# A linear-attention block in front of a gated unit: the product of k and v stands in TensorE, q streams through it, and x is born as [channel, token]

## The chip, the core and the metric

The kernel runs on one core of a Trainium2 chip. The metric is the device time of one execution in microseconds. A core has five engines with an instruction queue each: TensorE (PE in the profile, with its weight loads shown apart as PEld), VectorE (DVE), ScalarE (ACT), GpSimd (POOL) and SyncE (SP), which here only starts transfers. An engine takes its instructions in the order in which they were written, and waits at a semaphore where one needs another engine's result.

## What is computed

```python
def _attn_ref(q, k, v, g_norm):                       # (8, 8, 576, 64): batch, head, token, channel
    kv = np.einsum('bhsd,bhse->bhde', k, v)           # 64 x 64 for each head
    out = np.einsum('bhsd,bhde->bhse', q, kv)
    rms = np.sqrt(np.mean(out * out, axis=-1, keepdims=True) + 1e-06)
    return out / rms * g_norm

# x: (8, 576, 512), the heads side by side; w_val, w_out: (512, 512); conv_w: (5, 512)
def _moe_ref(x, w_val, conv_w, w_out):
    xp = np.concatenate([np.zeros((B, K - 1, D)), x], axis=1)
    gate_pre = sum(conv_w[k] * xp[:, k:k + S, :] for k in range(K))
    gate = 1.0 / (1.0 + np.exp(-gate_pre))
    return (gate * (x @ w_val)) @ w_out
```

All is in fp32 on the chip. q, k, v and g_norm come in fp32, the three weights in fp64, which the kernel narrows itself. `g_norm` and the root of 64 are folded into the weights, so that what is left of the norm is x times (sum of squares + 64 eps) to the power -1/2, for each token and head.

## The kernel before

A batch has 576 tokens and 512 channels. The second half of the work wants x with channels on the partitions, as `xT[128, 4, 576]` with a halo of four blocks in front of it, because the causal convolution then is four shifted multiply-adds along the free dimension. The first half makes x with tokens on the partitions. The steps of a batch:

- `load_half`, `load_tails`, `load_q` and `load_q_rows` bring k, v and q in through SP's queue. `kv_product` (L408) makes kv for two heads at a time, one in output columns 0 to 63 and one in 64 to 127 of TensorE's array. `kv_copy` (L418) puts each pair on the diagonal of a 128x128 block, `kvbd`.
- `turn_q` (L431, L434) turns q in blocks of 32 by 32 on DVE; for the first two batches `turn_q_rows` (L446) and `sort_q` do it on TensorE and ScalarE.
- `raw_product` (L485): for each of five chunks of tokens (four of 128, one tail of 64) four products in which 128 tokens of q stand as weights and `kvbd`, 128 columns, streams. The result is [token, channel] in one PSUM bank of two that have the tag `raw`; the bank is held until x has been made from it.
- `square` (L499, ScalarE), `sums` (L507, a reduction on DVE), `powers` (L513, `pow` on GpSimd) give the factor of each token and head; `normalise` multiplies with it, on DVE for batches 0 to 2 (L528), on ScalarE with eight instructions for a chunk (L524) from batch 3 on.
- x is turned to channels on partitions: with transposes on TensorE (`turn_x`, L538) and a copy (`keep_x`, L545) for the first two batches and every tail; else with block transposes on DVE (`turn_blocks`, L553) and four transfers from GpSimd's queue for each quarter (`move_blocks`, L561). `halo` (L568, GpSimd) fills the four blocks in front of it.
- the gate: `gate_start` (L572, ScalarE), four `gate_tap` (L578, DVE, each 128x576), `gate_end` (L585, the sigmoid on ScalarE), four times for a batch.
- the value product with w_val: `val_product` (L590) as eight groups of four plain products for the first two batches, from batch 2 on `val_fast` (L640), Strassen's scheme with seven products out of eight, whose partial results `x_sums` (DVE) and `val_keep` (ScalarE copies and DVE adds) make and collect. `gated` (L603) multiplies the gate in.
- the output product: `out_product` (L671, and L678 for the tails of two batches) or `fast_product` (L735), Strassen again, with `token_sums` and `fast_keep`; `store` sends the rows out.

The first products of the kernel wait for loads. `keep_warm` (L397) puts products of the identity into TensorE's queue in that time.

The order of the instructions on every engine comes from a planner that runs when the program is built. Each step has an engine, a time that its author expects (`"PE", 0.905`), a wished start, the steps it needs, and the buffers it takes and frees. `order` picks again and again the step that can start first. `SHIFTS` moves the wished starts of single steps. PSUM's eight banks are dealt out as `kv` 1, `raw` 2, `tp` 1 and `mm` 4. So the program holds the work of about three batches at once: while one batch's output product runs, the next one's value product and the one after's attention lie between its groups.

## Time and profile before

| | us |
|---|---|
| median of three runs | 333.09 (332.76 to 333.61) |
| the profiled execution, its own time | 333.21 |
| its span, first to last instruction | 331.4 |

| group | instructions | busy us | mean ns |
|---|---|---|---|
| raw products (L485), full chunks | 256 | 34.1 | 279 |
| raw products (L485), tails | 64 | 5.4 | 286 |
| transposes of x on TensorE (L538) | 48 | 8.1 | 277 |
| squares on ScalarE (L499), all | 40 | 22.5 | 561 |
| reductions on DVE (L507), all | 40 | 25.2 | 630 |
| powers on GpSimd (L513), all | 40 | 67.7 | 1697 |
| x on ScalarE (L524) | 180 | 39.6 | 342 |
| block transposes of x on DVE (L553) | 24 | 16.7 | 700 |
| transfers of x's blocks (L561) | 96 | 52.9 | 557 |

The clock granted to TensorE has a mean of 0.999 of the full one. An fp32 product shows as two MATMUL records and two LDWEIGHTS records. A record's duration reaches from its start to the end of a pipeline that the next record has entered long before, so the durations of a group overlap with those of the next: what a group takes of TensorE's time is read from the distance between starts. In the timeline a row is a merged run: start, length, engine, line, operation, tiles, shapes, count.

### The profile page before, as it was taken

What the parts mean: (1) busy time and instruction counts of PE and PEld (TensorE: products, weight loads), DVE (VectorE), ACT (ScalarE), POOL (GpSimd) and SP (SyncE); (2) the same over time, 40 slices, a digit from 0 to 9 for tenths busy, and PEclk for the clock granted to TensorE, in tenths of its full rate; (3) what the DMA queues carried; (4) which work ended last, traced back from release to release, by engine and by line L of the source; (5) the groups of instructions that cost most, each with busy time, mean ns of one, the idle gap of its engine ahead of it and who ended that gap; (6) DMA issues with size and microseconds to landing.
All of it is one profiled execution on the core that took longest, in us unless ns stands there. A gap on an engine that the chain in (4) does not pass through costs nothing.

```text
span 331.4 us, 6416 instructions
## 1 busy us (share of the span) xinstructions
PE 318.4 (96%) x2193; PEld 244.5 (74%) x2193; DVE 268.8 (81%) x479; ACT 185.8 (56%) x497; POOL 135.2 (41%) x178
## 2 busy tenths in 40 slices
PE   4989999999999999999999999999999999999993
PEld 4988877878755747587778758787885888888752
DVE  3277689799999729999999999999896697999601
ACT  3646965874365667675347848763676543534220
POOL 3006325303347969802568247777223274000000
PEclk9999999999999999999999999999999999999999
DMA  6999897597866886772976899465201235211233
GB/s 205 303 224 355 232 338 204 149 257 217 267 177 176 229 236 163 172 230 71 297 172 164 209 265 278 107 148 131 66 2 32 63 64 122 72 32 34 63 79 79
DMA packets 46014, 55.37 MB, mean 167 GB/s; under 512 B 15754, under 2 KB 36254, under 8 KB 45982
## 3 DMA queue, kind: packets, MB, share of 16 engines
q1 hardware_dynamic: 42558, 48.41, 53.6%
q0 software_dynamic: 3072, 6.30, 8.4%
q10 hardware_dynamic: 352, 0.26, 0.4%
q8 instruction: 17, 0.28, 0.4%
q14 instruction: 15, 0.12, 0.1%
HBM read 39.21 MB, written 9.44 MB: 147 GB/s over the span
## 4 chain that ended last, share of the span: by engine, by line
PE 76%; DVE 8%; DMA 7%; SPq 4%; ACT 2%; issue 2%; POOL 1%; DVEq 0%; ACTq 0%; POOLq 0%
PE va L640 12%; PE a L735 10%; PE raw L485 9%; PE out L671 8%; PE cb L735 8%; PE val L590 8%; PE vc L640 6%; PE out L678 4%; PE kv L408 4%; DVE gate L578 4%; PE vb L640 3%; DMA k<-in_k_dram 2%; DMA w_wval<-in_moe_w_val_dram 2%; PE xTps L538 2%; DMA vl<-in_v_dram 2%
## 5 line engine op out<-in xcount | busy, mean ns | idle before, releaser
L513 POOL TENSOR_TENSOR rt<-ss,mhalf 128x8 f32<-128x8 f32 (+1 forms) x40 | 67.7, 1697 | 113.4 <-DVE ss L507 113.4
L578 DVE SCALAR_TENSOR_TENSOR gate<-xT,cwT,gate 128x576 f32<-128x576 f32 x128 | 98.8, 808 | 0.1
L561 POOL DMA_DIRECT2D xT<-y x96 | 52.9, 557 | 20.8 <-PE vc L640 7.5
L524 ACT ACTIVATE x<-raw,rt 128x64 f32<-128x64 f32 x180 | 39.6, 342 | 7.5 <-POOL rt L513 7.5
L485 PEld LDWEIGHTS raw<-kvbd,qT 128*128 128x128 f32 (+1 forms) x320 | 35.4, 180 | 8.4 <-issue 4.7
L485 PE MATMUL raw<-kvbd,qT 128*128 128x128 f32 (+1 forms) x320 | 39.1, 280 | 0.9 <-DVE x L528 0.6
L507 DVE TENSOR_REDUCE ss<-sq 128x8 f32<-128x520 f32 (+1 forms) x40 | 25.2, 630 | 11.3 <-ACT sq L499 10.8
L590 PE MATMUL val<-xT,wval 128*128 128x288 f32 x128 | 33.2, 409 | 0.0
L499 ACT ACTIVATE sq<-raw 128x512 f32<-128x512 f32 (+1 forms) x40 | 22.5, 561 | 18.5 <-PE raw L485 18.2
L671 PE MATMUL out<-wout,gv 128*128 128x512 f32 x64 | 28.5, 595 | 0.0
L590 PEld LDWEIGHTS val<-xT,wval 128*128 128x128 f32 x128 | 23.5, 190 | 5.8
L640 PE MATMUL va<-xs,vsum 128*128 128x288 f32 x96 | 27.3, 407 | 0.0
L603 DVE TENSOR_TENSOR gv<-gv,gate 128x576 f32<-128x576 f32 x32 | 23.5, 747 | 4.1 <-ACT gate L585 1.8
L585 ACT ACTIVATE gate<-gate 128x576 f32<-128x576 f32 x32 | 21.5, 690 | 8.9 <-DVE gate L578 8.6
L572 ACT ACTIVATE gate<-xT,cwT 128x576 f32<-128x576 f32 x32 | 24.1, 778 | 1.6 <-DVE gv L603 1.1
L735 PE MATMUL a<-wsum,sums 128*128 128x256 f32 x96 | 24.9, 381 | 0.0
L408 PEld LDWEIGHTS kv<-v,k 128*64 128x64 f32 x512 | 17.6, 137 | 6.6 <-issue 4.6
L408 PE MATMUL kv<-v,k 128*64 128x64 f32 x512 | 20.6, 226 | 1.3 <-DMA vl<-in_v_dram 1.2
L671 PEld LDWEIGHTS out<-wout,gv 128*128 128x128 f32 x64 | 11.8, 190 | 13.2 <-issue 12.4
L640 PEld LDWEIGHTS va<-xs,vsum 128*128 128x128 f32 x96 | 18.0, 190 | 4.7
L744 DVE TENSOR_TENSOR ot<-cb,ot 128x256 f32<-128x256 f32 x24 | 10.0, 416 | 13.8 <-ACT ot L748 9.5
L553 DVE STREAM_TRANSPOSE y<-x 128x512 f32<-128x512 f32 x24 | 16.7, 700 | 4.2 <-ACT x L524 4.2
(109 smaller groups left out, 561.7 us busy)
## 6 DMA issues: line engine op xcount, KB each, us to landing
q<-in_q_dram SPq DMA_DIRECT2D x96, 140.0 KB, 4.1
out_dram<-ot SPq DMA_DIRECT2D x140, 64.0 KB, 1.7
v<-in_v_dram SPq DMA_DIRECT2D x16, 512.0 KB, 5.3
k<-in_k_dram SPq DMA_DIRECT2D x16, 512.0 KB, 7.0
xT<-y POOLq DMA_DIRECT2D x96, 64.0 KB, 2.8
q<-in_q_dram SPq DMA_DIRECT2D x4, 512.0 KB, 6.9
w_wval<-in_moe_w_val_dram SPq DMA_DIRECT2D x4, 512.0 KB, 7.8
w_wout<-in_moe_w_out_dram SPq DMA_DIRECT2D x4, 512.0 KB, 6.8
```

Source lines behind the costliest of these rows:

```text
L408: nc.tensor.matmul(kvp[r * D:(r + 1) * D, hp, :], st["k", b, half][:, h, j, :] if j < NJ else kl[:, 2 * hp + r, :], st["v", b, half][:, h, ...
L485: nc.tensor.matmul(raw[row * m:(row + 1) * m, col * P:(col + 1) * P], st["qT", b][:, hp, c * P:c * P + m], kv_bd[b % 2][:, hp, :], start=T ...
L507: nc.vector.reduce_sum(out=ss[:, 0:n], in_=st["sq", b, c][:, 0:n], axis=AX.X)
L513: nc.gpsimd.tensor_tensor(out=rt[:, 0:n], in0=st["ss", b, c][:, 0:n], in1=mhalf[:, 0:n], op=ALU.pow)
L524: nc.scalar.activation(out=x[:, cols], in_=st["raw", b, c][:, cols], func=AF.Copy, scale=st["rt", b, c][:, h:h + 1])
L561: nc.gpsimd.dma_start(out=xTs[b % 2][i * TB:(i + 1) * TB, :, first:first + P], in_=y[a * TB:(a + 1) * TB, i])
L572: nc.scalar.activation(out=gate[:], in_=xTs[b % 2][:, jt, HALO:SX], func=AF.Copy, scale=cwT[:, K - 1, jt:jt + 1])
L578: nc.vector.scalar_tensor_tensor(out=gate[:], in0=xTs[b % 2][:, jt, tap * TB:tap * TB + S], scalar=cwT[:, tap, jt:jt + 1], in1=gate[:], op ...
L590: nc.tensor.matmul(val[:], wval[:, kc, jt * P:(jt + 1) * P], xTs[b % 2][:, kc, HALO + n * SV:HALO + (n + 1) * SV], start=(kc == 0), stop=( ...
L640: nc.tensor.matmul(st[bank, "val", b, mj][:], weights_[:, k], tokens()[:, k], start=(n in (0, 1, 3) and k == 0), stop=(k == NK // 2 - 1), ...
L671: nc.tensor.matmul(po[:], gv[:, jt, first:first + P], wout[:, jt, :], start=(jt == 0), stop=(jt == NK - 1),)
L735: nc.tensor.matmul(st[bank, i, p], tokens()[:, k], weights_[:, k], start=(n < 2 and k == 0), stop=(k == NK // 2 - 1), skip_group_check=True)
```

## The change

- kv is kept as it comes from PSUM, `kvs[128, 4, 64]`, two heads above each other, instead of on diagonals. `head` deals the heads out so that the slots fit.
- `raw_product` swaps the operands: a head's 64x64 kv stands in TensorE, q streams in 288 columns (half of the tokens). A group of four products has its operands in both halves of the rows and its results in both halves of the columns, and two PSUM banks as its result. There are four groups for a batch: two halves of the tokens (`g`), two pairs of channel blocks (`p`). The result is [channel, token].
- `keep_raw` (ScalarE) copies it straight into `xT`; `square` (ScalarE) squares it from there.
- `sums`: four products with `fold`, a 128x32 matrix of ones, add the squares over a head's channels and leave each head's sum on 16 partitions. `root` (ScalarE, Sqrt), `inverse` and `exact` (DVE: a reciprocal and three scalar_tensor_tensor, of which the last ones are a Newton step) make the factor.
- `spread`: two products of 32 rows with `spread_` lead each head's factor to its 64 channels, and `normalise` (DVE) multiplies `xT` with it in place.
- `turn_x`, `keep_x`, `turn_blocks` and `move_blocks` are gone, and `turn_q` is one transpose instead of two.
- the tag `raw` is one tile of two banks instead of two tiles of one bank. It holds a raw group, a spread factor, or the sums of an output product at the end.
- the value products need `xT` by halves and pairs, not by chunks. All wished starts in `SHIFTS` are others.

```diff
@@ -200,30 +205,29 @@
     loads = ctx.enter_context(tc.tile_pool(name="loads", bufs=2))
     work = ctx.enter_context(tc.tile_pool(name="work", bufs=2))
     psum = ctx.enter_context(tc.tile_pool(name="psum", bufs=1, space=bass.MemoryType.PSUM))
-    BANKS = {"kv": 1, "raw": 2, "tp": 1, "mm": 4}
+    BANKS = {"kv": 1, "raw": 1, "tp": 1, "mm": 4}
 
     def ps(kind, shape, name):
         return psum.tile(shape, FP32, tag=kind, bufs=BANKS[kind], name=name)
 
     plan = Planner({
-        "k0": 1, "k1": 1, "v0": 1, "v1": 1, "tails": 2, "q": 3, "w64": 3, "y": 2, "wexp": 2,
-        "kv": 1, "kvbd": 2, "qT": 2, "tp": 1, "raw": 2, "mm": 4, "sq": 2, "ss": 3, "rt": 3,
-        "x": 2, "xT": 2, "gate": GATES, "xs": 4, "gv": GVS, "ot": 3,
-    }, by_batch=("tails", "kvbd", "xT", "gv"))
+        "k0": 1, "k1": 1, "v0": 1, "v1": 1, "tails": 2, "q": 3, "w64": 3, "wexp": 2,
+        "kv": 1, "kvs": 2, "qT": 2, "tp": 1, "raw": 1, "mm": 4, "sq": 4, "rt": 2,
+        "xT": 2, "gate": GATES, "xs": 4, "gv": GVS, "ot": 3,
+    }, by_batch=("tails", "kvs", "xT", "gv"))
 
 
     tails = [[const.tile([P, H, D], FP32, name=f"{n}l{i}") for n in ("k", "v")] for i in range(2)]
-
-    kv_bd = [const.tile([P, HP, P], FP32, name=f"kvbd{i}") for i in range(2)]
+    kvs = [const.tile([P, HP, D], FP32, name=f"kvs{i}") for i in range(2)]
     ident = const.tile([P, P], FP32, name="ident")
-    mhalf = const.tile([P, H], FP32, name="mhalf")
...
@@ -235,20 +239,23 @@
     EVEN, ODD = slice(0, NK // 2), slice(NK // 2, NK)
 
     def set_up():
-        for n, bias in enumerate((127.0 - 1023.0, 255.0, 255.0 * (1 << 23))):
+        for n, bias in enumerate((127.0 - 1023.0, 255.0, 255.0 * (1 << 23), D * EPS)):
             nc.vector.memset(biases[:, n:n + 1], bias)
         make_identity(nc, ident[:])
         for pair in tails:
             for t in pair:
                 nc.gpsimd.memset(t[T:P], 0.0)
-        for t in kv_bd:
-            nc.vector.memset(t[:], 0.0)
-        nc.vector.memset(mhalf[:], -0.5)
+        nc.vector.memset(fold[:], 0.0)
+        for r in range(2):
+            nc.vector.memset(fold[r * D:(r + 1) * D, r * TB // 2:(r + 1) * TB // 2], 1.0)
+            nc.vector.reduce_sum(
+                out=picks[:, r:r + 1],
+                in_=ident[:].rearrange("p (g i) -> p i g", i=TB)[:, r * TB // 2:r * TB // 2 + 1, :], axis=AX.X)
+            nc.vector.tensor_copy(
+                spread_[:, r * D:(r + 1) * D], picks[:, r:r + 1].broadcast_to((P, D)))
         for t in xTs:
...
+    def head(s, w):
+
+        return s // 2 * 4 + 2 * w + s % 2
...
     def kv_copy(b):
-        for r in range(2):
-            rows = slice(r * D, (r + 1) * D)
-            nc.scalar.copy(out=kv_bd[b % 2][rows, :, rows], in_=st["kvps", b][rows])
+        nc.scalar.copy(out=kvs[b % 2][:], in_=st["kvps", b])
...
     def turn_q(b, hp):
-
-        q, qT = st["q", b, hp], new_qT(b)[:, hp, :]
-        if b < TURNED_X:
-            nc.vector.transpose(out=qT, in_=q[:, :, 0:TB])
-            return
-        nc.vector.transpose(
-            out=qT[:, 0:SF].rearrange("p (c a t) -> p c a t", c=NJ, a=HB),
-            in_=q[:, 0:NJ * HB, 0:TB].rearrange("p (a c) t -> p c a t", c=NJ))
-        nc.vector.transpose(out=qT[:, SF:S], in_=q[:, NJ * HB:NB, 0:TB])
+        nc.vector.transpose(out=new_qT(b)[:, hp, :], in_=st["q", b, hp][:, :, 0:TB])
...
-    def raw_product(b, c):
...
+    def of_x(b, g, p):
+
+        return xTs[b % 2][:, 2 * p:2 * p + 2, HALO + g * SV:HALO + (g + 1) * SV]
+
+    def raw_product(b, g, p):
+        st["raw", b, g, p] = raw = ps("raw", [P, 2, 512], f"raw{b}_{g}{p}")
+        for u in range(2):
+            for w in range(2):
+                rows = slice(w * D, (w + 1) * D)
+                nc.tensor.matmul(
+                    raw[u * D:(u + 1) * D, w, 0:SV], kvs[b % 2][rows, 2 * p + u, :],
+                    st["qT", b][rows, 2 * p + u, g * SV:(g + 1) * SV], start=True, stop=True)
+
+    def keep_raw(b, g, p):
+        nc.scalar.copy(out=of_x(b, g, p), in_=st["raw", b, g, p][:, :, 0:SV])
+
+    def square(b, g, p):
+        st["sq", b, g, p] = sq = work.tile([P, 2, SV], FP32, tag="sq", bufs=4, name=f"sq{b}_{g}{p}")
+        nc.scalar.activation(out=sq[:], in_=of_x(b, g, p), func=AF.Square)
+
+    def sums(b, g):
+        st["ss", b, g] = ss = ps("tp", [P, SV], f"ss{b}_{g}")
+        for kc in range(NK):
             nc.tensor.matmul(
+                ss[kc * TB:(kc + 1) * TB, :], fold[:], st["sq", b, g, kc // 2][:, kc % 2, :],
+                start=True, stop=True)
+
+    def root(b, g):
+        st["root", b, g] = t = work.tile([P, SV], FP32, tag="root", bufs=2, name=f"root{b}_{g}")
+        nc.scalar.activation(out=t[:], in_=st["ss", b, g][:], func=AF.Sqrt, bias=biases[:, 3:4])
+
+    def inverse(b, g):
+        st["rt", b, g] = rt = work.tile([P, SV], FP32, tag="rt", bufs=2, name=f"rt{b}_{g}")
+        t = st["root", b, g]
+        nc.vector.reciprocal(rt[:], t[:])
+        nc.vector.scalar_tensor_tensor(
+            out=t[:], in0=st["ss", b, g][:], scalar=D * EPS, in1=rt[:], op0=ALU.add, op1=ALU.mult)
+
+    def exact(b, g):
+        rt, t = st["rt", b, g], st["root", b, g]
+        nc.vector.scalar_tensor_tensor(
+            out=t[:], in0=t[:], scalar=-0.5, in1=rt[:], op0=ALU.mult, op1=ALU.mult)
+        nc.vector.scalar_tensor_tensor(
+            out=rt[:], in0=t[:], scalar=1.5, in1=rt[:], op0=ALU.add, op1=ALU.mult)
+
+    def spread(b, g, p):
+        st["norm", b, g, p] = norm = ps("raw", [P, 2, 512], f"norm{b}_{g}{p}")
+        for w in range(2):
+            rows = slice((2 * p + w) * TB, (2 * p + w + 1) * TB)
+            nc.tensor.matmul(
+                norm[:, w, 0:SV], spread_[rows, :], st["rt", b, g][rows, :], start=True, stop=True,
+                tile_position=(rows.start, 0))
+
+    def normalise(b, g, p):
+        x = of_x(b, g, p)
+        nc.vector.tensor_tensor(out=x, in0=x, in1=st["norm", b, g, p][:, :, 0:SV], op=ALU.mult)
...
+        for n, (g, p) in enumerate(GROUPS):
+            t = first + n * 1.25 * step
+            key = b, g, p
+            plan.add(
+                "PE", 0.55, t, raw_product, *key, needs=parts + [("kvs", b)], gives=[("raw", key)],
+                takes=[("raw", ("raw", key))], frees=[("kvs", b), ("qT", b)],
+            )
+            plan.add(
+                "ACT", 0.62, t + 0.8, keep_raw, *key, needs=[("raw", key)], gives=[("kept raw", key)],
+                takes=[("xT", b)] if n == 0 else [], frees=[("raw", ("raw", key))],
+            )
+            plan.add(
+                "ACT", 0.62, t + 1.5, square, *key, needs=[("kept raw", key)], gives=[("sq", key)],
                 takes=[("sq", key)],
             )
             plan.add(
+                "PE", 0.3, t + 6.0, spread, *key, needs=[("rt", b, g)], gives=[("norm", key)],
+                takes=[("raw", ("norm", key))], frees=[("rt", (b, g))],
+            )
+            plan.add(
+                "DVE", 0.68, t + 6.5, normalise, *key, needs=[("norm", key)], gives=[("xT", b, g, p)],
+                frees=[("raw", ("norm", key))],
+            )
+        for n, g in enumerate((1, 0)):
+            t = first + (2 * n + 1) * 1.25 * step + 2.2
+            key = b, g
+            plan.add(
+                "PE", 0.5, t, sums, *key, needs=[("sq", (b, g, p)) for p in range(2)], gives=[("ss", key)],
+                takes=[("tp", key)], frees=[("sq", (b, g, p)) for p in range(2)],
+            )
+            plan.add(
+                "ACT", 1.6, t + 0.5, root, *key, needs=[("ss", key)], gives=[("root", key)], takes=[("rt", key)],
+            )
+            plan.add(
+                "DVE", 0.78, t + 2.0, inverse, *key, needs=[("root", key)], gives=[("inverse", key)],
+                frees=[("tp", key)],
+            )
+            plan.add(
+                "DVE", 0.76, t + 2.8, exact, *key, needs=[("inverse", key)], gives=[("rt", b, g)],
+            )
         plan.add(
+            "POOL", 1.5, first + 5 * step, halo, b, needs=[("xT", b, 1, p) for p in range(2)],
```

## The prediction

> **What bounds the kernel now.** I read the page's busy times first, then the windows of the stages, then TensorE's timeline, then the chain of waits. The busy times:
>
> ```profile
> PE 318.4 (96%) x2193; PEld 244.5 (74%) x2193; DVE 268.8 (81%) x479; ACT 185.8 (56%) x497; POOL 135.2 (41%) x178
> ```
>
> TensorE is busy for 96% of the span, but some of that is filler: the products of the identity that `keep_warm` issues while the first loads come. The windows show where the filler ends (columns: stage, its length, then busy time and instructions of PE, PEld, DVE, ACT, POOL, clock, DMA):
>
> ```profile
> 40.00:52.30 12.30, 11.75 (x132) 9.27 (x132) 10.96 (x18) 8.75 (x17) 3.05 (x2) 1.00 0.75 258
> 52.30:120.00 67.70, 67.70 (x474) 47.66 (x473) 60.60 (x107) 40.24 (x100) 33.26 (x38) 1.00 0.82 223
> 120.00:200.00 80.00, 79.15 (x511) 57.20 (x509) 73.84 (x129) 49.07 (x144) 43.66 (x56) 1.00 0.74 193
> 200.00:280.00 80.00, 79.55 (x447) 63.31 (x446) 70.65 (x118) 48.24 (x145) 44.12 (x65) 1.00 0.40 98
> 280.00:331.40 51.40, 46.07 (x202) 35.58 (x200) 31.81 (x55) 15.68 (x37) 0.00 (x0) 0.99 0.24 62
> ```
>
> From the first value product (39.93 us) to 280 us TensorE has 1.8 us without work, in the last stage 5.3. No other engine is near that. So the forecast is a sum over TensorE's queue from the first value product on. What the reader should take from the timeline is the distance between starts, because ends are modelled and overlap:
>
> ```profile
> 9.91 3.71 PE L446 MATMUL qTps<-ident,q 128*64 128x128 f32 x64
> 13.55 5.18 PE L397 MATMUL kv<-ident 128*128 128x128 f32 x44
> ...
> 25.88 4.43 PE L485 MATMUL raw<-kvbd,qT 128*64 128x128 f32 x40
> 30.15 0.38 PE L538 MATMUL xTps<-ident,x 128*128 128x128 f32 x2
> 30.46 1.97 PE L446 MATMUL qTps<-ident,q 128*64 128x128 f32 x32
> 32.36 0.66 PE L538 MATMUL xTps<-ident,x 128*128 128x128 f32 x4
> ...
> 43.28 2.21 PE L590 MATMUL val<-xT,wval 128*128 128x288 f32 x8
> 45.42 1.75 PE L485 MATMUL raw<-kvbd,qT 128*64 128x128 f32 x16
> ```
>
> and from the chain of waits, a long run of value products with nothing between them:
>
> ```profile
> 67.45 9.70 PE val L590 x40
> ```
>
> Each fp32 product is two records. Three readings follow.
> (a) A 288-column record takes 9.70 / 40 = 0.2425 us in a row.
> (b) Products with 64 output columns, alternating between the halves of the array (qTps), run two at a time: 64 records take 13.55 - 9.91 = 3.64 us and 32 take 32.36 - 30.46 = 1.90, so 32 more cost 1.74, which is 0.109 for a pair; a 128-column record of raw alone costs about as much (0.115 below). Column tiles really overlap.
> (c) Going into and out of such tiles is not free. 1.90 - 1.74 leaves 0.16 us inside one visit, and the value group of 8 records between two visits takes 45.42 - 43.28 = 2.14 instead of 8 x 0.2425 = 1.94, so 0.10 on each side. A visit between two full-array groups costs 0.16 + 2 x 0.10 = 0.36 us beyond its streaming: 0.18 for each change of array shape.
>
> **What the Trainium skill says.** "TensorEngine Tiling (Array Packing)", Key Properties, has it that tiles work in parallel and that a change of tiling mode drains TensorE; (b) and (c) agree, the page gives no price and the trace gives 0.18. "TensorE: Matmul & The Clock Gate", Part 3, reports 3.07x for four row tiles of 32 rows and 2.38x for three column tiles, all in streams of 512; no row tile side by side with another is in the trace of before, so this is the only support for that half of the change. "ScalarE: Activation LUTs", What ACT_TABLE_LOAD costs, gives 1.28 us for a load and some 1.38 for the drain at each change of set; the trace has two loads, each 1.283 us.
>
> **The change part by part**, on TensorE from the first value product on.
>
> *Removed.* One batch's raw products: from 25.88 to 30.15, 4.27 us with one visit's inner 0.16, so 4.11 streaming (32 full records at about 0.115, 8 tail records in column pairs). Seven batches: 28.8. The transposes of x (L538): batch 1 has four full chunks at 0.44 (the chain's group of four) and a tail at 0.22, batches 2 to 7 a tail each: 1.98 + 1.3 = 3.3. Sum 32.1.
>
> *Added.* A raw group is four 64x64 products of 288 columns in four tiles, eight records; four at a time gives 2 x 0.2425 = 0.485. Seven batches times four groups: 28 x 0.485 = 13.6. `sums` is four 128x32 products in four column tiles: again two record times, 14 x 0.485 = 6.8. `spread` is two products of 32 rows in two row tiles: two record times, 30 x 0.485 = 14.6 (two of batch 0's come after the first value product). Sum 35.0. Streaming alone is thus 2.9 us more than before: swapping what stands and what streams halves the raw products, and the two new kinds of product with ones eat the gain.
>
> *Shape changes.* I counted the places in TensorE's instruction order, from the first value product on, where the array shape differs from that of the instruction before: 52 before (kv, raw tails, the single output chunks), 169 after, since 72 short groups are sprinkled between value and output products. 117 more at 0.18 is 21.1 us. This is the largest term. The bounds of it: if the row-only shape of `spread` pays nothing, some 45 changes go, -8 us; if tiles of 64x64 drain for longer (up to the 0.27 us that a matmul record lasts), 117 x 0.09 = +10.5. I take 0.18, the only measured value.
>
> TensorE together: 2.9 + 21.1 = +24.0 us.
>
> *Other engines, each against a TensorE that is now slower.* DVE loses the reductions (L507, 25.2 us), the block transposes (L553, 16.7), x (L528, 9.3) and the second transpose of q (4.8, while the first grows by about 2). It gains 64 operations of 288 elements (reciprocal and three scalar_tensor_tensor, at about 0.42 from the 0.45 of the 288-wide adds in L647) and 32 multiplies of 576 at about 0.74: 27 + 24. Net -3, so no bound. If the reciprocal takes four times a plain pass, 16 x 1.3 = +21 on DVE, which at 81% it could just carry. ScalarE loses x (39.6), squares (22.5), L545 (8.2) and half of kv_copy (3), and gains 32 copies and 32 squares of 576 at about 0.67 (43), 16 roots of 288 at about 0.5 (8), and table loads: 21 in its order instead of 2, 19 x 1.283 = 24.4. Net about +2 on an engine at 56%. GpSimd loses the powers (67.7) and 96 transfers with 6.3 MB, and keeps the halos. All this is covered by TensorE's queue; if that cover is gone, the exposed piece is the wait of a product for the ScalarE copy in front of it, behind a table load.
>
> *The start.* Until the first value product the time is set by loads and a chain through ScalarE and DVE. After, v comes behind k, q and two weights (about 4.6 MB; at the 0.23 to 0.28 MB/us of the first stages that is a landing near 21 to 24, now 23.25), then copies, squares, root, inverse and spread for the second half of the tokens only. I count 0, +-3.
>
> *The end.* The last output products, stores and the 5.3 us without work there stay as they are: 0.
>
> Sum: 331.4 + 24.0 = 355.4 of span; the profiled execution's own time, 333.21, is 1.8 above its span and 0.1 above the median 333.09. So **357 us**.
>
> **Rivals.**
> 1. *Row groups don't run side by side.* Then raw runs two at a time (28 x 0.485 more) and spread one at a time (30 x 0.485 more): +28.1, 385 us. For it: no such overlap is in the trace. Against it: the two products of each pair write to different PSUM banks and different rows, and the skill's measurement.
> 2. *Table loads and the single raw buffer reach TensorE.* A sequence va, copy on ScalarE, va again leaves the copy about one group's time (0.97); a table load of 1.28 and a root of 0.5 fit in only when they fall between. If half of the 19 added loads stick out, +12: 369 us. The planner's 0.6 for the sigmoid step holds no load, which speaks for it; a TensorE that lags its plan speaks against it.
> 3. *Faster: the shape changes vanish in the queue.* The mechanism is TensorE's weight loads: if the first load of each tile group is pulled ahead under the full-array product in front of it, a group costs what the planner's list writes (0.55, 0.5, 0.3). Then 28 x 0.55 + 14 x 0.5 + 30 x 0.3 = 31.4 is added, 32.1 and fourteen changes of the raw tails (2.5) are removed, and the 1.8 us without work go with GpSimd's powers: -5, 328 us. It decides from 34.6 / 72 = 0.48 us for a whole short group, shape changes included. Against it: reading (c).
>
> **How the numbers follow.** The forecast 0.6 (own range 349 to 366: 8 below for a free row shape, 9 above for longer drains), rival 1 0.14, rival 2 0.15, rival 3 0.11. The likeliest gives 357. The range, 342 to 378, leaves out rival 1 and most of rival 3. About 0.3% is what a measurement of this kernel can tell from no change; rival 3 is faster with 0.09 and within it with 0.02, and small errors of the sum add 0.01 to no change: 0.09, 0.03, 0.88.
>
> **What would show it.** The starts of the eight records of a raw group: four within some tens of ns, then four 0.24 later, is the forecast; two and two is rival 1. A value group of 8 records next to a tile group at 2.04 to 2.14 instead of 1.94 shows the changes, and 1.94 is rival 3. In the windows from 60 to 280 PE busy at 98% or more says that the sum decides; idle time before va or cb with ScalarE as releaser is rival 2. The forecast is wrong if TensorE is busy and the groups are short, or if the value products start later than 45 us.

## The result and the profile after

The changed kernel takes **365.23 us** (median; 364.97 to 366.06) where the kernel before takes 333.09: a ratio of 1.0968, 95% interval 1.0933 to 1.1004. The span of its profiled execution is 364.3 us, 32.9 more than before. The forecast was 357.

The page's busy times and the shares of the chain of waits, of the kernel after:

```profile
PE 341.9 (94%) x2341; PEld 223.1 (61%) x2341; DVE 294.0 (81%) x475; ACT 190.0 (52%) x352; POOL 18.8 (5%) x42
...
PE 80%; DVE 7%; ACT 4%; DMA 4%; issue 2%; SPq 2%; DVEq 0%; ACTq 0%
```

TensorE is still the engine that bounds. It has 23.5 us more of work. GpSimd has shrunk from 135.2 to 18.8 us, and the time rose all the same. VectorE, for which the forecast had 3 us less, has 25.2 more.

The windows of TensorE's time from the first value product on, first of the kernel before, then of the kernel after (columns: stage, its length, then busy time and instructions of PE, PEld, DVE, ACT, POOL, clock, share of the DMA engines, GB/s):

```profile
39.93:130.00 90.07, 89.52 (x647) 63.13 (x646) 78.04 (x134) 56.40 (x138) 44.77 (x51) 1.00 0.79 219
130.00:210.00 80.00, 79.13 (x521) 59.30 (x519) 76.99 (x137) 49.41 (x151) 42.86 (x58) 1.00 0.79 208
210.00:300.00 90.00, 89.57 (x482) 71.77 (x483) 79.48 (x132) 49.49 (x138) 36.45 (x52) 1.00 0.30 73
300.00:331.40 31.40, 26.07 (x114) 18.89 (x112) 13.36 (x24) 6.75 (x16) 0.00 (x0) 0.99 0.23 60
```

```profile
40.82:130.00 89.18, 87.94 (x588) 48.62 (x586) 83.47 (x122) 52.39 (x87) 4.36 (x8) 1.00 0.67 175
130.00:210.00 80.00, 79.09 (x519) 48.79 (x514) 71.05 (x109) 46.90 (x83) 3.48 (x8) 1.00 0.52 139
210.00:300.00 90.00, 87.49 (x572) 57.16 (x570) 81.76 (x127) 46.62 (x85) 5.36 (x10) 1.00 0.30 81
300.00:364.30 64.30, 55.80 (x242) 41.74 (x240) 35.66 (x62) 17.90 (x40) 0.88 (x2) 0.98 0.22 54
```

Each stage's length less its PE busy time is what TensorE had nothing to do. Added up, the 32.9 us fall into four parts, which the following sections use:

| part | before | after | difference | forecast |
|---|---|---|---|---|
| start of the first value product | 39.93 | 40.82 | +0.9 | 0 |
| TensorE busy from there on | 284.3 | 310.3 | +26.0 | +24.0 |
| TensorE without work from there to 300 us | 1.9 | 4.7 | +2.8 | 0 |
| the same after 300 us | 5.3 | 8.5 | +3.2 | 0 |

So four fifths of the loss are the term that was forecast, and 6.9 us are waits and a start for which the sum had nothing.

The timeline of TensorE in the kernel after (columns: start, duration, engine, line, operation, out<-in, array rows*columns, shape, records):

```profile
53.33 0.72 PE L488 MATMUL raw<-qT,kvs 64*64 64x288 f32 x8
53.98 0.69 PE L502 MATMUL ss<-sq,fold 128*32 128x288 f32 x8
54.60 2.21 PE L561 MATMUL val<-xT,wval 128*128 128x288 f32 x8
56.74 0.72 PE L488 MATMUL raw<-qT,kvs 64*64 64x288 f32 x8
...
60.84 0.69 PE L502 MATMUL ss<-sq,fold 128*32 128x288 f32 x8
61.46 0.75 PE L528 MATMUL norm<-rt,spread 32*128 32x288 f32 x4
62.15 2.21 PE L561 MATMUL val<-xT,wval 128*128 128x288 f32 x8
64.28 0.76 PE L528 MATMUL norm<-rt,spread 32*128 32x288 f32 x4
64.97 2.21 PE L561 MATMUL val<-xT,wval 128*128 128x288 f32 x8
```

By the distances of the starts, a raw group holds TensorE for 0.65 us (53.33 to 53.98), a group of sums for 0.62, a spread for 0.69. Two record times side by side would be 0.485; the rest, 0.14 to 0.20, is the cost of the visit inside it. The value group between two visits lasts 2.14 (54.60 to 56.74, 62.15 to 64.28) and not the 1.94 of eight records in a row. That is the forecast's reading (c) again.

The same timeline, cut so short that the eight records of the raw group at 53.33 come in two rows:

```profile
53.33 0.47 PE L488 MATMUL raw<-qT,kvs 64*64 64x288 f32 x4
...
53.63 0.42 PE L488 MATMUL raw<-qT,kvs 64*64 64x288 f32 x4
```

Four records last 0.47 us together where one lasts 0.45, so they start within 0.02 us of each other; the other four start 0.29 later. Four tiles do run at a time, which is the first sign that the forecast asked for (it named 0.24 between the two sets).

The row tiles were the half of the change that no trace of before could show. All records of one spread, in the kernel after (columns: durations of minimum, median, maximum in ns, then the first and the last start in us):

```profile
L528 PE MATMUL norm<-rt,spread x4: 401/453/505, 61.5 to 61.8; 32*128 32x288 f32 x4
```

Four records of 0.2425 us one after the other would put the last start 0.73 us behind the first; it lies some 0.3 behind. The two row tiles run side by side, and rival 1 (385 us) is out.

The costliest of the new groups of instructions in the kernel after, shapes kept apart (columns: line, engine, operation, out<-in, count, busy us, mean ns, then the idle time just ahead of it and its releaser):

```profile
L513 DVE RECIPROCAL rt<-root 128x288 f32<-128x288 f32 x16 | 31.1, 1944 | 4.0 <-ACT root L508 4.0
L528 PE MATMUL norm<-rt,spread 32*128 32x288 f32 x128 | 24.1, 452 | 2.7 <-DVE rt L521 2.6
L508 ACT ACT_TABLE_LOAD x10 | 12.8, 1283 | 0.2
L556 ACT ACT_TABLE_LOAD x10 | 12.8, 1283 | 0.2
...
L521 DVE SCALAR_TENSOR_TENSOR rt<-root,rt 128x288 f32<-128x288 f32 x16 | 7.3, 458 | 0.6
```

One reciprocal of 288 elements takes 1.944 us, 4.2 times the scalar_tensor_tensor of the same shape. The forecast had taken 0.42 and named four times a plain pass as the bound. The idle column of the spread says that TensorE waited 2.6 us for the end of this chain; the experiments below ask how much that is in the whole.

### The profile page after: what moved, and what is told of

It reads as the page before. It is cut to its first block, busy times and chain, and to the rows that moved or that the text cites. A ratio compares the mean times of both kernels' runs of the same rounds, so it can differ in the third digit from the quotient of the medians.

```text
span 364.3 us, 6293 instructions
## 1 busy us (share of the span) xinstructions
PE 341.9 (94%) x2341; PEld 223.1 (61%) x2341; DVE 294.0 (81%) x475; ACT 190.0 (52%) x352; POOL 18.8 (5%) x42
## 4 chain that ended last, share of the span: by engine, by line
PE 80%; DVE 7%; ACT 4%; DMA 4%; issue 2%; SPq 2%; DVEq 0%; ACTq 0%
PE va L611 11%; PE val L561 9%; PE a L708 8%; PE out L642 8%; PE cb L708 6%; PE vc L611 6%; PE norm L528 6%; PE kv L419 5%; PE raw L488 5%; PE cba L708 5%; PE out L649 4%; DMA q<-in_q_dram 4%; PE vb L611 3%; DVE rt L513 2%; PE ss L502 2%
## 5 line engine op out<-in xcount | busy, mean ns | idle before, releaser
L513 DVE RECIPROCAL rt<-root 128x288 f32<-128x288 f32 x16 | 31.1, 1944 | 4.0 <-ACT root L508 4.0
L539 POOL COPY xT<-xT 128x124 f32<-128x124 f32 x32 | 16.0, 528 | 283.6 <-DVE xT L534 283.6
L534 DVE TENSOR_TENSOR xT<-xT,norm 128x576 f32<-128x576 f32 x32 | 23.9, 747 | 7.2 <-PE norm L528 7.0
L528 PE MATMUL norm<-rt,spread 32*128 32x288 f32 x128 | 24.1, 452 | 2.7 <-DVE rt L521 2.6
L493 ACT COPY xT<-raw 128x576 f32<-128x576 f32 x32 | 20.3, 635 | 11.4 <-PE raw L488 10.9
L488 PE MATMUL raw<-qT,kvs 64*64 64x288 f32 x256 | 22.9, 428 | 0.0
L497 ACT ACTIVATE sq<-xT 128x576 f32<-128x576 f32 x32 | 21.8, 680 | 0.4
L708 PE MATMUL a<-wsum,sums 128*128 128x256 f32 x72 | 19.0, 386 | 0.0
L435 DVE STREAM_TRANSPOSE qT<-q 128x576 f32<-128x576 f32 x24 | 18.4, 769 | 0.0
L528 PEld LDWEIGHTS norm<-rt,spread 32*128 32x128 f32 x128 | 9.7, 182 | 14.1 <-issue 6.7
```

Of the source, the lines that this page charges most:

```text
L488: nc.tensor.matmul(raw[u * D:(u + 1) * D, w, 0:SV], kvs[b % 2][rows, 2 * p + u, :], st["qT", b][rows, 2 * p + u, g * SV:(g + 1) * SV], sta ...
L513: nc.vector.reciprocal(rt[:], t[:])
L528: nc.tensor.matmul(norm[:, w, 0:SV], spread_[rows, :], st["rt", b, g][rows, :], start=True, stop=True, tile_position=(rows.start, 0))
L534: nc.vector.tensor_tensor(out=x, in0=x, in1=st["norm", b, g, p][:, :, 0:SV], op=ALU.mult)
L708: nc.tensor.matmul(st[bank, i, p], tokens()[:, k], weights_[:, k], start=(n < 2 and k == 0), stop=(k == NK // 2 - 1), skip_group_check=True)
```

## The experiments

Two theories stood against each other at first. **A**: the time is TensorE's, and nearly all of it is shape changes at about 0.18 us each, since the streaming taken away and the streaming added cancel. **B**: the changes cost little (or TensorE hides them), and the time comes from what hangs on the small products: the reciprocal, the table loads, the one raw buffer.

### Shape changes alone, in the kernel before

48 products of 64 columns whose result nobody reads are put behind the fourth and the sixth of each set of seven Strassen products. In the first kernel they use 64 of the array's columns, which makes 134 shape changes where there were 52; in the second they use all 128, and there are still 52.

```diff
+    def visit():
+        nc.tensor.matmul(
+            st["spare"].rearrange("p h d -> p (h d)")[0:64, 0:64], ident[:, 0:64], ident[:, 0:64],
+            start=True, stop=True)
...
+        if n in (3, 5):
+            visit()
```

> The kernel before, with 48 extra products of the identity in TensorE's queue, each 64 output columns wide and 64 columns long, put behind the fourth and sixth group of every seven-product set of batches 2 to 7. Their results are used by nobody. The shape changes in TensorE's order, from the first value product on, go from 52 to 134. Theory (a change of array shape costs TensorE 0.18 us, and TensorE's queue sets the time): 48 x 0.11 us of streaming and 82 x 0.18 us of changes, +20.0, so 353 us. Rival (the changes vanish under the neighbours, what costs is the streaming alone): +5, 338 us. Rival (the change only costs where the queue is not already waiting): something between, with idle time of TensorE shrinking.

> As the run with 48 extra products 64 columns wide, but 128 output columns wide, so that the array keeps its shape; 52 changes as in the kernel before. Theory: streaming alone, 48 x 0.11 = +5.3, 338 us; the difference to the run with narrow products, about 15 us over 82 changes, is the price of the changes. Rival (what costs is a further product, not the shape): both runs the same, within 2 us.

Measured: 349.3 us (ratio 1.0515, 1.0437 to 1.0593) and 341.75 us (1.0255, 1.0214 to 1.0297). The two differ only in the columns used. The timelines of TensorE around such a product, first with 64 columns, then with 128:

```profile
160.99 1.13 PE L645 MATMUL vb<-xT,wval 128*128 128x288 f32 x4
162.05 0.33 PE L401 MATMUL kv<-ident 128*64 128x64 f32 x2
162.31 1.24 PE L645 MATMUL va<-xs,vsum 128*128 128x288 f32 x4
163.38 1.13 PE L645 MATMUL vc<-xT,vsum 128*128 128x288 f32 x4
```

```profile
160.68 1.13 PE L645 MATMUL vb<-xT,wval 128*128 128x288 f32 x4
161.65 0.33 PE L401 MATMUL kv<-ident 128*128 128x64 f32 x2
161.82 1.19 PE L645 MATMUL va<-xs,vsum 128*128 128x288 f32 x4
162.84 1.13 PE L645 MATMUL vc<-xT,vsum 128*128 128x288 f32 x4
```

From the start of `vb` to the start of `vc` pass 163.38 - 160.99 = 2.39 us with the narrow product between, and 162.84 - 160.68 = 2.16 with the wide one; two groups of four records alone are 8 x 0.2425 = 1.94. An inserted narrow product thus costs 0.45 us and a wide one 0.22. The narrow one's pieces: `vb` is held 0.09 longer (1.06 instead of 0.97), the visit lasts 0.26 and `va` 1.07. Its two records of 64 columns stream for some 0.11 (the 128 columns of a raw record in the forecast), which leaves about 0.34 for two changes, **0.17 each**, if the narrow product is charged with nothing but its streaming.

The comparison that was named beforehand gives less. The two kernels were to differ by about 15 us and differ by 7.6, which is 0.09 us for each of the 82 changes, or 0.11 by TensorE's busy time. The wide product is the reason: it costs 0.22 and not the 0.11 of its columns. TensorE's weight loads at the same places show both what such a product meets and what a change of shape does, first with 64 columns, then with 128:

```profile
162.05 0.19 PEld L401 LDWEIGHTS kv<-ident 128*64 128x64 f32 x2 [0.39 <-issue]
```

```profile
161.41 0.43 PEld L401 LDWEIGHTS kv<-ident 128*128 128x128 f32 x2
161.76 0.79 PEld L645 LDWEIGHTS va<-xs,vsum 128*128 128x128 f32 x4
```

The wide product keeps the shape, and its first load starts at 161.41, 0.24 us ahead of its first record (161.65) and under the last record of `vb`. The narrow one changes the shape, and its first load starts together with its first record at 162.05, after 0.39 us without a load. The raw group at 56.74 in the changed kernel has the same 0.39 ahead of its loads. So what is lost at a change of shape is, in these places, a load that isn't pulled ahead: the mechanism of rival 3 does not happen there. Behind the wide product the loads come 0.11 us apart (its second at 161.65, the first of `va` at 161.76), longer than a record of 64 columns; that this makes its 0.22 is likely and was not tried by itself.

The pair thus puts a change at 0.09 to 0.17 us, depending on what a short product is charged with. It is not nothing, which refutes theory B's claim that changes are free: the same number of products costs twice as much when it uses half of the array.

The totals were +16.3 us for an expected +20 and +8.7 for +5. TensorE's busy time from the first value product on rose by 18.0 us with narrow products and by 9.3 with wide ones (0.19 a product). Its idle time fell by 1.2 and 0.4, and the first value product came 1.2 and 0.4 us earlier (38.74 and 39.54).

### Fewer changes for more streaming, in the changed kernel

Two parts of the change are undone alone: the raw products use the full array again (kv of two heads on the diagonal of a 128x128 block; 121 changes instead of 169), or the spreading does (a 128x128 selection instead of 32 rows; 124 changes). The output is the same. The excerpts show the products alone; the first edit also puts kv on its diagonal and deals the heads out to suit, the second also builds the selection at the start.

```diff
...
-            for w in range(2):
-                rows = slice(w * D, (w + 1) * D)
-                nc.tensor.matmul(
-                    raw[u * D:(u + 1) * D, w, 0:SV], kvs[b % 2][rows, 2 * p + u, :],
-                    st["qT", b][rows, 2 * p + u, g * SV:(g + 1) * SV], start=True, stop=True)
+            nc.tensor.matmul(
+                raw[:, u, 0:SV], kvs[b % 2][:, 2 * p + u, :],
+                st["qT", b][:, 2 * p + u, g * SV:(g + 1) * SV], start=True, stop=True)
...
```

> The changed kernel with only the raw products in the full array: kv of two heads stands on a diagonal as before, q streams in 288 columns, two products for a group instead of four in four tiles. Streaming of a group 0.97 instead of 0.485 us, shape changes 121 instead of 169. Theory (a change costs 0.18): +13.6 for 28 groups, -8.6 for 48 changes, so +5: 370 us. Rival (changes are nearly free, the loss of the changed kernel lies in waits): +13.6, 379 us. If a change costs more than 0.28 us, it is faster than the changed kernel, below 365.

```diff
...
-                norm[:, w, 0:SV], spread_[rows, :], st["rt", b, g][rows, :], start=True, stop=True,
-                tile_position=(rows.start, 0))
+                norm[:, w, 0:SV], sel[:, 2 * p + w, :], st["rt", b, g][:], start=True, stop=True)
```

> The changed kernel with only the spreading in the full array: a 128x128 selection for each block of channels, with zeros in the rows of the other heads, stands instead of 32 rows of ones. Streaming of a group 0.97 instead of 0.485, shape changes 124 instead of 169. Theory (two row tiles run side by side, and a change costs 0.18): +14.6 - 8.1 = +6, 371 us. Rival (row tiles don't run side by side): no more streaming than now, 8 us fewer for changes, 357 us. Rival (a row-only shape changes for free): +14.6, 380 us.

Measured: 371.12 us (1.1132, 1.1075 to 1.1189) and 374.1 us (1.1234, 1.1185 to 1.1282). TensorE's timeline of the second:

```profile
64.22 1.24 PE L532 MATMUL norm<-rt,sel 128*128 128x288 f32 x4
65.29 2.10 PE L564 MATMUL val<-xT,wval 128*128 128x288 f32 x8
67.23 1.13 PE L532 MATMUL norm<-rt,sel 128*128 128x288 f32 x4
68.20 2.10 PE L564 MATMUL val<-xT,wval 128*128 128x288 f32 x8
```

With the full array the value group beside a spread is back at 1.94 us (65.29 to 67.23), and the spread lasts 0.97 (67.23 to 68.20) instead of 0.69. This pair of times is the exchange rate: 0.28 us more of streaming for 0.20 less at the neighbour, a net loss of 0.08.

The busy time of TensorE makes it a price. For the raw products the streaming grows by 28 x 0.485 = 13.6 us and 48 changes go; busy from the first value product on grows by 5.2 (315.5 against 310.3), so a change is worth (13.6 - 5.2) / 48 = 0.175. For the spreading it is 30 x 0.485 = 14.6, 45 changes and +6.6: (14.6 - 6.6) / 45 = 0.178. Two edits give the same price for a visit in place, with all that belongs to it. Each rests on one profile, and three executions of the changed kernel lie 1.1 us apart, which is 0.02 us of price for 48 changes; that the two agree more closely is luck. The rest of the 8.9 us of the second is mostly the start: the first value product comes at 42.66 us instead of 40.82. Half of this is the two spreads of batch 0 ahead of it, which last 1.14 and 1.16 us instead of 0.68 each. The added building of the selection can be the cause of the other half; it was not tried apart. Both edits also show that the tiles that run side by side do earn more than their changes cost: without them the kernel would be slower still.

### The reciprocal and the table loads

Three kernels leave a part of the work out. The first has Identity in place of Sqrt, so the root is left out, and with it all table loads but two. The second has a scalar_tensor_tensor in place of the reciprocal, so that is left out. The third leaves out both.

```diff
-        nc.scalar.activation(out=t[:], in_=st["ss", b, g][:], func=AF.Sqrt, bias=biases[:, 3:4])
+        nc.scalar.activation(out=t[:], in_=st["ss", b, g][:], func=AF.Identity, bias=biases[:, 3:4])
...
-        nc.vector.reciprocal(rt[:], t[:])
+        nc.vector.scalar_tensor_tensor(
+            out=rt[:], in0=t[:], scalar=0.5, in1=t[:], op0=ALU.mult, op1=ALU.add)
```

> The changed kernel with Identity instead of Sqrt in the root step: the root is left out, so that the factor is not the norm's. ScalarE's table loads drop from 20 to 2. Theory (the loads lie under TensorE's queue): 0 to -3 us, 362 to 365 us. Rival (the loads hold TensorE): -8 or more, below 357 us, with less idle time of TensorE behind ScalarE.

> The changed kernel with a scalar_tensor_tensor of the same 288 elements where the reciprocal stands: the reciprocal is left out. 16 x (1.944 - 0.458) = 23.8 us less for DVE. Theory (DVE has room, most is covered): the two reciprocals before the first value products (3 us, on the chain of waits there) and a part of TensorE's 13.2 us without work after 40 us go: -3 to -6, 359 to 362 us. Rival (DVE's queue sets the pace in the steady stages): -10 or more, below 355 us.

> Both left out, the root and the reciprocal. Theory (what remains of the loss is TensorE's own queue): -4 to -8, 357 to 361 us, TensorE busy for 97% from the first value product on, still some 25 us above the kernel before. Rival (latency of the long norm chain is the cause): back to within 10 us of the kernel before, below 343 us.

Measured: 362.83 (ratio 1.0890, 1.0869 to 1.0911), 362.06 (1.0870, 1.0843 to 1.0896) and 358.85 us (1.0774, 1.0750 to 1.0798): 2.4, 3.2 and 6.4 less than the changed kernel. Nineteen loads of 1.283 us are 24.4 us of ScalarE, and sixteen reciprocals 16 x (1.944 - 0.474) = 23.5 us of VectorE, where 0.474 is the substitute; a tenth and a seventh of that reach the end. The windows of the kernel with neither:

```profile
38.61:130.00 91.39, 91.39 (x608) 51.03 (x607) 78.63 (x125) 49.00 (x88) 4.36 (x8) 1.00 0.72 186
130.00:210.00 80.00, 79.83 (x514) 49.51 (x513) 67.48 (x114) 37.12 (x72) 3.69 (x9) 1.00 0.51 140
210.00:300.00 90.00, 89.84 (x587) 59.73 (x586) 76.57 (x129) 38.98 (x80) 6.45 (x12) 1.00 0.28 73
300.00:356.50 56.50, 47.98 (x208) 36.39 (x206) 29.29 (x51) 15.90 (x37) 0.00 (x0) 0.99 0.23 57
```

Here TensorE starts at 38.61 instead of 40.82 and has 0.3 us without work up to 300, instead of 4.7. What is left against the kernel before is 309.0 - 284.3 = 24.7 us of TensorE's own queue, and the forecast's sum for that was 24.0. Of the 24.7, 0.9 us are three products of the identity that `keep_warm` puts behind the first value product (43.33 to 44.26); the changed kernel has them too, the kernel before has none. After 300 us there are still 8.5 us without work, as in the changed kernel: that part has nothing to do with the root or its inverse.

TensorE's waits part in the same way. In the changed kernel `va` and `cb` wait 2.7 us for copies on ScalarE, which is the sign that the forecast named for rival 2. Without the reciprocal this wait stays, without the table loads it is gone. The 2.6 us in which spreads wait for VectorE stay without the table loads (2.7) and are gone without the reciprocal.

How the reciprocal gets to the start is in the chain of waits of the kernel after, in order of time, its short pieces left out (columns: start, duration, what):

```profile
17.64 3.64 PE qTps L447 x64
21.28 2.36 PE kv L419 x80
32.38 1.87 DVE rt L513
40.14 1.87 DVE rt L513
44.91 1.31 PE kv L419 x40
48.48 2.14 PE val L561 x8
```

Two reciprocals of the first batch stand in the chain itself, ahead of the value products. In the kernel with the substitute the first value product starts at 38.59, 2.2 us earlier, which is more than half of what that kernel gains.

### Taking changes away: a re-planned order, and the order kept

The opposite test is to make fewer changes of the same work. First the planner of the kernel before was given the kv products of two head pairs as one step (38 changes).

```diff
-    def kv_product(b, hp):
+    def kv_product(b, i):
+        for hp in range(2 * i, 2 * i + 2):
+            kv_pair(b, hp)
...
-                "PE", 0.68, kv_first + 1.5 * hp, kv_product, b, hp,
+                "PE", 1.31, kv_first + 3.0 * i, kv_product, b, i,
...
```

> The kernel before with the kv products of two pairs of heads as one step of the planner: ten products more in a row, 38 shape changes instead of 52; the planner orders anew. Theory (0.18 for a change, TensorE bound): -2.5 us, 330.6, if the new order brings no new waits. Rival (the new order matters more than the changes): anything from -2 to +8, with idle time of TensorE to show for it.

Measured: 356.43 us (1.0695, 1.0663 to 1.0728), a plain miss of the expectation and outside the range of its rival too. Two of its windows:

```profile
130.00:210.00 80.00, 72.44 (x532) 55.69 (x530) 74.67 (x133) 51.69 (x165) 46.28 (x56) 0.97 0.78 209
210.00:300.00 90.00, 81.18 (x374) 61.40 (x375) 65.45 (x107) 39.89 (x110) 33.38 (x48) 0.93 0.23 59
```

From 130 to 300 us TensorE has 16.4 us without work, where the kernel before has 1.3, and the granted clock falls to 0.97 and 0.93 in these stages. From the first value product on TensorE's busy time is 290.1 us, 5.8 more than before, although 14 changes are gone; how much of that is the clock was not separated. One different step gave the planner another order for everything behind it. So this run says nothing of shape changes; the new plan cost 23 us, over two thirds of the loss under study.

Therefore the plan was then left as it is, and only the finished list edited: the first kv product of a pair is moved down to stand ahead of the second.

```diff
-        for start, step in plan.order():
+        steps = plan.order()
+        for at in [n for n, (_, s) in enumerate(steps) if s["fn"] is kv_product and s["args"][1] % 2 == 0][::-1]:
+            b, hp = steps[at][1]["args"]
+            to = next(n for n, (_, s) in enumerate(steps) if s["fn"] is kv_product and s["args"] == (b, hp + 1))
+            late = steps.pop(at)
+            steps.insert(to - 1, (steps[to - 1][0], late[1]))
+        for start, step in steps:
```

> The kernel before, its planned order kept: the plan is made as before, and afterwards the first kv product of each pair (head pairs 0 and 2) is moved down the finished list to stand directly ahead of the second (1 and 3). Same instructions, shape changes of TensorE 44 in place of 52. Theory (a change costs 0.17 to 0.18 us, and nothing else of the order matters this much): 8 x 0.175 = 1.4 us less, 331.7 us, TensorE idle as before. Rival, after the run in which the planner was given the pairs as one step and the time rose by 23 us: kv products in pairs are themselves bad (a longer block ahead of the raw products): 336 us or more. If the time rises as there, the re-planned order wasn't the cause of that rise.

> The changed kernel with the same edit of the finished list: shape changes 156 in place of 169, the same instructions. Theory: 13 x 0.175 = 2.3 us less than the changed kernel, 363.0 us, ratio about 1.090. Rival (changes cost nothing by themselves, the time comes of the small products' own length): 365.2 us, no difference. Rival (pairs are bad): 368 us or more.

Measured: 334.47 us (1.0049, 1.0027 to 1.0071) and 367.59 us (1.1047, 1.1020 to 1.1073), both slightly slower. The sentence "the same instructions" in these expectations was wrong. The fill products at the start are reckoned from the starts in the list, and the move drew in 13 more of them in the kernel before and 10 in the changed one (`kv<-ident`: 122 records instead of 96, 120 instead of 100). The two runs decide nothing, and the move was made once more for batches 3 to 7 alone, which leaves the fill products as they were.

> The same move in the kernel before, for batches 3 to 7 alone, so that the first 60 us and their fill products stay as they are (in the earlier run the move also drew in 13 more fill products at the start, 3.3 us of TensorE). Shape changes 46 in place of 52. Theory: 6 x 0.175 = 1.0 us less TensorE work; but the earlier run also showed a product of the normalised rows waiting 1.4 us for ScalarE in the stretch from 130 to 210 us, behind a pair that came late; where this stays, 333.5 us, no difference. Rival (pairs are bad by themselves): 336 us.

> The same move in the changed kernel, for batches 3 to 7 alone. Shape changes 156 in place of 169, the same instructions. Theory: 13 x 0.175 = 2.3 us less, 363.0 us, ratio about 1.090; less of it where TensorE waits more than the 13 us it idles after 40 us now. Rival (changes cost nothing): 365.2 us.

Measured: 333.26 us (1.0020, 1.0005 to 1.0035) and 364.81 us (1.0965, 1.0938 to 1.0992). Neither is a gain that could be told from none, and the 363.0 that was expected of the second did not come. The last line of the second's windows, from its first value product (40.56) to its end (363.3), with the sum of each engine's busy time:

```profile
sum 322.74, PE 308.64 PEld 195.66 DVE 271.65 ACT 163.45 POOL 14.09; mean PE 77.16 PEld 48.92 DVE 67.91 ACT 40.86 POOL 3.52
```

TensorE's busy time is 308.6 instead of 310.3, 1.7 of the 2.3 us that 13 changes should be worth, and its idle time is 322.74 - 308.64 = 14.1 instead of 13.2. So some half of what the work went down by came back as waiting, perhaps because a kv product that comes later makes what hangs on it later; the waits were not traced to it. In the kernel before, 6 changes fewer, which should be worth 1.0 us, leave busy time within 0.1 us. Both effects are about as large as what one execution differs from the next by (1.1 us in the changed kernel), so taking changes away has neither confirmed the price nor refuted it. No kernel of this study beats the kernel before.

## Why the prediction was right, and where it was short

- **The bound and the mechanism: right.** TensorE's queue sets the time; its busy time from the first value product on rose by 26.0 us where 24.0 was forecast, and by 24.7 in the kernel without root and reciprocal. An error of 0.02 us in the price of a change is 2.3 us in this sum, so an agreement within 1 us is in part luck.
- **Streaming, +2.9: agrees.** The groups last 0.65, 0.62 and 0.69 us, which is the forecast's two record times plus the inner part of a visit. Row tiles and column tiles run side by side.
- **Shape changes, 117 x 0.18 = 21.1: right as the price of a visit.** The price was read from a few places in the trace of before. It came out as 0.175 and 0.178 from two edits of the changed kernel, which change exactly these visits. Products that do nothing else gave 0.17 by their streaming and 0.09 against products of the full array, so how much of a visit is the change of shape itself, and how much any short product costs, is less sure than the sum. (The upper end of the forecast's own range takes 9 us for longer drains where its working has 10.5; the result is inside either.) That the row-only shape of the spread is free (8 us less) is refuted by the spread at 0.69 and its neighbour at 2.14.
- **VectorE, "Net -3, so no bound": the term that was mis-sized.** The reciprocal was put at about 0.42 us and takes 1.944, so VectorE got 25.2 us more. The forecast had named this case and held that VectorE "could just carry" it. It carries most of it: 3.2 us reach the end, in good part at the start, through the chain of the first batch.
- **Table loads, hidden: nearly.** The count (21) and the duration (1.283, as the section What ACT_TABLE_LOAD costs of the Trainium skill's page "ScalarE: Activation LUTs" has it) were right. The 1.38 us for a drain that the prediction quotes from that section do not show: ten loads have 0.2 us of idle time of ScalarE ahead of them, and after 19 of the 20 loads behind the start the next activation begins 0.01 us later. Of 24.4 us, 2.4 reach the end, not the 12 of rival 2. The raw buffer of one tile leaves no trace at the raw products, whose idle time ahead is 0.0; the last stage, below, may be another matter.
- **The start, 0 within 3: right in size.** +0.9 with the reciprocal and -1.3 without it (38.59 against 39.93).
- **"The last output products, stores and the 5.3 us without work there stay as they are": wrong by 3.2 us.** The timeline of the last stage, TensorE's waits alone:

```profile
324.57 1.13 PE L708 MATMUL cba<-wout,sums 128*128 128x256 f32 x4 [0.60 <-DVE ot L717]
341.77 1.13 PE L708 MATMUL cb<-wsum,sums 128*128 128x256 f32 x4 [1.15 <-DVE sums L682]
349.45 1.13 PE L708 MATMUL cba<-wsum,sums 128*128 128x256 f32 x4 [0.51 <-ACT ot L719]
351.91 1.13 PE L708 MATMUL cba<-wsum,sums 128*128 128x256 f32 x4 [0.46 <-ACT ot L723]
```

The output products of the end now wait for copies and sums, together 2.7 us in four places, where the kernel before has 0.3 in one; and from the end of the last product to the end of the span pass 5.8 us (364.3 - 358.55) instead of 4.9. The same four waits and the same 5.8 us stand in the kernel without root and reciprocal. Three of the waits are at the tile `cba`, which sits in the one raw buffer and holds what were two tiles before. Whether that tile or the other order is the reason was not tried and stays open.

So a forecast span of 355.4 became 364.3 by 2.0 us of TensorE's work (0.9 of it the products of the identity), 3.2 of the last stage, and 3.7 of start and waits. Leaving out the root and the reciprocal takes 6.4 us off the median. Between the two profiled spans (364.3 and 356.5) it is 7.8: 2.2 of start, 4.3 of waits, and 1.3 of TensorE's work after the first value product, for which I have no cause.

## What to carry to other kernels

Tiles that use a part of TensorE's array do run side by side, but count the visits before the streaming: each small group put between full-array products cost about 0.35 us beyond its streaming here, whatever it computed, so 0.485 us of work was billed as 0.85. When such groups replace larger ones, compare record times plus a price for each change of shape (0.18 in this kernel), and ask whether several groups can stand together. And measure a new step of a generated plan with the order kept, because a re-planned order moved the kernel before by 7%, and the same pairs in the kept order by 0.5% at most.

## What the runs showed of the hardware that was not expected

- A reciprocal of 128x288 in fp32 on VectorE takes 1.944 us, the scalar_tensor_tensor of that shape 0.458.
- In the places shown, where the array shape stays, the first weight load of a product starts 0.24 us ahead of its record (161.41 and 161.65); where it changes, both start together (162.05), after 0.39 us without a load.
- A full-array product of 64 columns between products of 288 costs 0.22 us and not the 0.11 of its columns. The loads around it come 0.11 us apart; that they are the reason was only argued.
- Nineteen table loads, 24.4 us of ScalarE, cost the kernel only 2.4 us; ScalarE is busy for 52% of the span.
